# A hand-written order of operations in a fused attention and feed-forward kernel: the stretch behind the first batch's last scores is ordered anew, with weight sums in halves on two engines and two pairs turned by DMA

## The chip, the cores and the metric

The kernel runs on one core of a Trainium2 chip. The core has five engines with a queue of instructions each: TensorE (PE: matrix products; its weight loads are shown apart as PEld), VectorE (DVE), ScalarE (ACT), GpSimd (POOL) and SyncE (SP, which here issues most DMAs). Each queue runs in its own order and waits on semaphores for the others. The metric is device time in microseconds (us) for one execution.

## The reference

Eight batches of twelve heads, sequence 448, head size 64. Queries and keys are divided by their norms, the attention is a softmax of their products over tau, and its result goes through a feed-forward layer with a hard-swish:

```python
q_n = q / (norm(q) + 1e-06);  k_n = k / (norm(k) + 1e-06)
attn = softmax(q_n @ k_n.T / tau)
x = (attn @ v) as [3584 tokens, 768]
h = x @ w_in                       # 768 x 2048
g = h * clip(h + 3, 0, 6) / 6
out = g @ w_out                    # 2048 x 768
```

## The kernel before

The work is cut into 48 pairs of heads, six pairs to a batch. A pair i needs its queries and keys squared (SQ), the squares summed (RE), norms made of the sums (NO), inputs multiplied by them (NM), and the result turned so that the head's 64 values lie on partitions (TR by TensorE, XD by a transposing DMA); then copies of queries and keys (CQ, CK, CS), scores in four groups (SC), exponentials (EX), products with the values (VA) and a division (FI). The finished pair is turned back into the layout of x, by matmuls against an identity (BK, then a copy CX) or by a DMA: XB for one pair, XP for two. When six pairs of a batch are there, sixteen units of the first product (U: `mm1_unit`, L560) make g, each with a ScalarE step (UA) and a VectorE product (UV); the output units (`mm2_unit`, L606, six for batch 0; `product_unit`, L720, and `single_unit`, L810, later) make the result. An output unit of the first kind is sixteen matmuls, a bank of PSUM, and a copy into o (L624 on ScalarE, L626 on VectorE), which a DMA stores.

TensorE's work of the later batches uses fewer products by a Strassen-like scheme (L652 on). It needs sums of quarters of w_out: sums 1, 6 and 7 go to tiles of their own, y3 and y4 overwrite the right and the left columns of w_out in place (`weight_sums`, L673; one token, WS). So y3 may only run when the first three output units of batch 0, which read the right half, are done, and y4 after the last three. Before the change, all of these sums run on VectorE, sum 7 and y4 in two halves, the others whole.

The order of the first 18 pairs is written out by hand as text, `PLAN` (L21): each token is an operation, then its numbers, and often the engine (v VectorE, a ScalarE, p GpSimd) and a part. Instructions enter their engine's queue in the order of the tokens. DP and D are dummy matmuls (L921, L916). W issues the next of eight weight loads from GpSimd's queue: four pieces of w_in, then four of w_out (L907). LQ and LV load queries or keys and values from SyncE's queue. The tile `big` holds the raw inputs in seven places that come around, so a load waits for the normalisation of the item seven before. From pair 18 on (`FIRST`) a loop sets the order (L996 to L1050). Scores, first-layer units and output units share six PSUM banks in a ring (`next_bank`, L157): a matmul into a bank waits until whoever read its last content is done.

The change's own names: `norms` (L244) takes four ScalarE steps, a logarithm, a half power by Exp, a logarithm of that plus epsilon and an Exp of its negative; `back` (L483) and `copy_x` (L497) turn a pair by TensorE; `back_two` (L514) turns two by one DMA; `weight_sums` (L673); `vcast` (L278) turns values to bf16; `copy_k` (L350) and `copy_k3` (L364) copy keys out of PSUM.

Of the kernel before, what the change touches and what calls it, by code (L numbers as in the profile page):

```python
# [10 lines left out]
AF = mybir.ActivationFunctionType  # L11
# [3 lines left out]
EPS = 1e-6  # L15
# [42 lines left out]
]  # L58


# [1 line left out]
def kernel(  # L62
# [10 lines left out]
    nc = tc.nc  # L73
    B, H, S, D = q.shape
# [29 lines left out]
    KC = FCN // 2  # L104
# [34 lines left out]
    def raw_buffer(j):  # L139
# [4 lines left out]
    n2s = [const.tile([128, 2, 14], FP32, name=f"n2{i}", tag=f"n2{i}") for i in range(2)]  # L144
    rs = [
        [const.tile([128, 2, 14], FP32, name=f"{x}{i}", tag=f"{x}{i}") for x in ("ln", "nr", "le", "r")]
        for i in range(2)
    ]
# [13 lines left out]
    engines = {"v": nc.vector, "p": nc.gpsimd, "a": nc.scalar, "s": nc.sync}  # L162
    issued = set()

    def needs(*what):
        for w in what:
            assert w in issued or any(x < 0 for x in w[1:] if isinstance(x, int)), w
# [76 lines left out]
    def norms(d, *items):  # L244

        needs(("NM", 2 * d - 4), ("NM", 2 * d - 3))
        items = items or (0, 1)
        for x in items:
            needs(("RE", 2 * d + x))
        it = slice(items[0], items[-1] + 1)  # L250
        ln, nr, le, r = (t[:, it, :] for t in rs[d % 2])
        nc.scalar.activation(out=ln, in_=n2s[d % 2][:, it, :], func=AF.Ln)
        nc.scalar.activation(out=nr, in_=ln, func=AF.Exp, scale=0.5)
        nc.scalar.activation(out=le, in_=nr, func=AF.Ln, bias=EPS)
        nc.scalar.activation(out=r, in_=le, func=AF.Exp, scale=-1.0)  # L255
        for x in items:
            issued.add(("NO", d, x))

# [411 lines left out]
            return wide[n % 2], wide[2]  # L670
        return wide_late[2 * (n - LOOP) : 2 * (n - LOOP) + 2]

    def weight_sums(what, c0, n):  # L673

        w = w_out_sb[:, :, :].rearrange("p (c k) m -> p c k m", k=2)[:, c0 : c0 + n]
        b11, b12, b21, b22 = (w[:, :, k, m] for k in range(2) for m in (LEFT, RIGHT))
        for x in {"y3": "16", "y4": "17"}.get(what, ""):
            assert all((x, c) in summed for c in range(c0, c0 + n))
        o, x, y, op = {
            "1": (b11, b11, b22, ALU.add),  # L680
            "6": (b11, b11, b12, ALU.add),
            "7": (b21, b21, b22, ALU.add),
            "y3": (b12, b12, b22, ALU.subtract),
            "y4": (b21, b21, b11, ALU.subtract),
        }[what]
        if what in w_sum:
            o = w_sum[what][:, c0 : c0 + n, :]
        nc.vector.tensor_tensor(out=o, in0=x, in1=y, op=op)
        summed.update((what, c) for c in range(c0, c0 + n))

    def half(b, t, k):
# [146 lines left out]
    def halved(x):  # L838
        return [(weight_sums, x, c, KC // 2) for c in (0, KC // 2)]

    def products(text):
# [18 lines left out]
    APART = {(n, y) for n in range(len(PAIRS)) for x, y in (("5a", "3"), ("2a", "4")) if f"{x}.{n}" in " ".join(TURNS.values()).split()}  # L860
    side = {
        18: [(weight_sums, "y4", KC // 2, KC // 2)], 19: sums(0, "62"), 20: sums(0, "1"),
        21: sums(1, "75"), 22: sums(1, "621"),
        25: sums(2, "75"), 26: sums(2, "62"), 27: sums(2, "1"), 28: [(g_left, 2)], 29: sums(2, "e"),
# [7 lines left out]
    for b in range(2, B - 1):  # L872
        first = firsts(b, *range(FCN))
        for n, x in enumerate([0, 3, 3, 3, 3, 2]):
# [6 lines left out]
            x = 0 if n == 1 else 1 if n in (0, 5) and i > FIRST else 2  # L881
# [54 lines left out]
    def finish_units(e):  # L936
        post[e].pop(0)()

    def whole_units(n, engines="av"):
# [4 lines left out]
                    finish_units(e)  # L944

    OPS = {
        "LQ": load_qk, "LV": load_v, "W": next_weights, "SQ": square, "RE": reduce, "NO": norms,
        "NM": normalise, "VC": vcast, "TR": transposes, "XD": crossbar, "XB": back_crossbar, "XP": back_two, "CQ": copy_q, "CK": copy_k, "CS": copy_k3, "SC": scores,
        "EX": exps, "VA": values, "FI": finish_values, "BK": back, "CX": copy_x, "U": unit, "UA": lambda: finish_units("a"), "UV": lambda: finish_units("v"),
        "GL": g_left, "WS": lambda x, *h: weight_sums(str(x), *((h[0] * KC // 2, KC // 2) if h else (0, KC))), "UU": whole_units, "D": busy, "DP": busy_pv, "OPEN": open_ring,  # L950
    }

    def do(op, *args):
        OPS[op](*args)
        key = (op,) + tuple(a for a in args if isinstance(a, int))
        if op not in ("RE", "NM", "LQ"):
            issued.add(key[:3] if op == "SC" else key)

    def run(text):
        for t in text.split():  # L960
            op, *args = t.split(".")
            do(op, *(int(a) if a.lstrip("-").isdigit() else a for a in args))
# [20 lines left out]
    SC = [psum_s.tile([128, 2, 512], FP32, name=f"SC{n}", tag=f"SC{n}") for n in range(2)]  # L983
# [10 lines left out]
    if FIRST + 6 < NP:  # L994
        do("LQ", FIRST + 6)
    for i in range(FIRST, NP):  # L996
# [5 lines left out]
        def prepare(*what):  # L1002
            for op, n, *args in what:
                if n < (NP // 2 if op in ("NO", "LV") else NP):
                    do(op, n, *args)
# [27 lines left out]
        n = 2  # L1033
# [59 lines left out]
```

## Time and profile before

| | us |
|---|---|
| median of three runs | 405.38 (405.06 to 406.32) |
| profiled execution, whole | 405.02 |
| its span | 403.2 |
| TensorE busy | 394.5 |
| VectorE busy | 286.4 |
| ScalarE busy | 266.2 |
| GpSimd busy | 233.2 |

The span runs from the first to the last recorded instruction; the execution's own time has some 1.8 us around it. A stretch by stretch view gives each engine's busy time (x its instructions), the granted TensorE clock, the busy share of the DMA engines (several DMAs in flight count as more than 1) and GB/s. In the stretches that the change touches:

```profile
core 0: us, PE busy (x) PEld busy (x) DVE busy (x) ACT busy (x) POOL busy (x), PEclk, DMA share, GB/s
...
62.00:72.00 10.00, 10.00 (x123) 6.26 (x121) 7.94 (x19) 8.20 (x20) 5.92 (x4) 1.00 1.24 241
72.00:82.00 10.00, 10.00 (x83) 5.17 (x81) 8.38 (x14) 7.35 (x19) 4.64 (x7) 1.00 0.88 141
82.00:92.00 10.00, 10.00 (x103) 5.41 (x102) 5.90 (x11) 8.05 (x17) 6.76 (x7) 1.00 0.80 125
92.00:102.00 10.00, 10.00 (x95) 6.02 (x93) 7.45 (x12) 7.35 (x19) 4.15 (x6) 1.00 1.12 242
102.00:112.00 10.00, 10.00 (x90) 6.16 (x89) 9.60 (x14) 5.96 (x16) 2.33 (x2) 1.00 0.94 171
112.00:117.00 5.00, 3.99 (x41) 2.20 (x39) 5.00 (x4) 2.60 (x7) 4.86 (x5) 1.00 0.81 238
```

A row of a timeline gives the start, the time, the engine, the line, the operation with its tiles, its shapes and how many were merged; in brackets the engine's idle time before it and who ended that.

### The profile page before, as it was taken

Reading aid. Unit: us, or ns where it says so; the run is one execution under the profiler, and the core shown is the slowest. Engines: PE = TensorE matmul, PEld = TensorE weight load, DVE = VectorE, ACT = ScalarE, POOL = GpSimd, SP = SyncE. Lnnn points to the kernel's source line nnn. Section 1 sums busy time; section 2 is a strip of 40 time slices with the busy share of each in tenths; the row PEclk is TensorE's granted clock in tenths of the full one; section 3 lists DMA queues with packets and bytes.
Section 4 is the critical chain, followed back from the end, with each engine's and each line's share of the span. In section 5 each row is a group of like instructions: output and inputs, shape, how many; then the busy total and the mean of one; then the engine's idle time right before and its main releaser. Section 6 shows DMA issues by size and latency. Waiting matters only on the chain.

```text
span 403.2 us, 9617 instructions
## 1 busy us (share of the span) xinstructions
PE 394.5 (98%) x3696; PEld 233.7 (58%) x3696; DVE 286.4 (71%) x501; ACT 266.2 (66%) x609; POOL 233.2 (58%) x228
## 2 busy tenths in 40 slices
PE   7999999999989999999999999999999999999996
PEld 5666556555655556555555556555565556555564
DVE  6898768766998676776857878687656666644663
ACT  6899998787557686776758768668648755224230
POOL 7899664562294996489386875776665500510070
PEclk9999999999999999999999999999999999999999
DMA  8999989989989559885989659986864523130133
GB/s 290 308 241 276 200 249 239 144 126 221 193 204 231 120 119 228 176 224 130 181 214 210 134 143 171 183 193 145 191 150 82 112 46 67 40 79 20 27 73 99
DMA packets 91566, 65.32 MB, mean 162 GB/s; under 512 B 56064, under 2 KB 89984, under 8 KB 91520
## 3 DMA queue, kind: packets, MB, share of 16 engines
q1 hardware_dynamic: 87408, 58.02, 62.8%
q0 software_dynamic: 3712, 6.29, 9.1%
q8 instruction: 29, 0.48, 0.5%
q10 hardware_dynamic: 400, 0.39, 0.3%
q14 instruction: 17, 0.14, 0.1%
HBM read 47.19 MB, written 11.01 MB: 144 GB/s over the span
## 4 chain that ended last, share of the span: by engine, by line
PE 94%; DVE 3%; DMA 1%; POOL 1%; ACT 0%; issue 0%; SPq 0%; DVEq 0%
PE M L566 24%; PE M L739 17%; PE PV L455 13%; PE Y L566 6%; PE M L415 6%; PE Z L566 5%; PE Y L739 4%; PE Z L739 4%; PE M L613 3%; PE M L819 2%; PE Z L415 2%; PE PV L921 2%; PE Z L819 1%; PE Y L415 1%; PE SC L415 1%; DMA big<-in_q_dram 1%
## 5 line engine op out<-in xcount | busy, mean ns | idle before, releaser
L433 ACT ACTIVATE at<-M 128x448 bf16<-128x448 f32 x200 | 99.6, 565 | 17.7 <-PE M L415 15.5
L566 PE MATMUL M<-xT,w_in_sb 128*128 128x448 bf16 x522 | 110.7, 353 | 0.0
L566 PEld LDWEIGHTS <-w_in_sb 128*128 128x128 bf16 x768 | 71.9, 98 | 62.5 <-issue 2.6
L267 POOL TENSOR_TENSOR nrm<-big,r 128x896 bf16<-128x896 f32 (+1 forms) x48 | 79.4, 1658 | 26.7 <-ACT r L255 18.5
L581 DVE SCALAR_TENSOR_TENSOR gT<-u,M 128x448 bf16<-128x448 bf16 x76 | 46.8, 618 | 35.6 <-ACT u L575 35.3
L455 PEld LDWEIGHTS <-at 128*128 128x128 bf16 (+1 forms) x1536 | 54.8, 97 | 24.1 <-issue 14.8
L224 POOL TENSOR_TENSOR big<-big 128x896 f32<-128x896 f32 (+3 forms) x39 | 63.8, 1639 | 8.0 <-DMA big<-in_k_dram 4.1
L575 ACT ACTIVATE u<-M 128x448 bf16<-128x448 f32 x87 | 48.8, 561 | 29.5 <-PE M L566 29.1
L455 PE MATMUL PV<-vx,at 128*128 128x65 bf16 (+1 forms) x1536 | 64.3, 194 | 0.2 <-DVE on L476 0.2
L236 DVE TENSOR_REDUCE n<-big 128x14 f32<-128x896 f32 (+1 forms) x50 | 51.8, 1040 | 3.9 <-ACT big L222 3.4
L372 POOL COPY km<-tT 64x128 bf16<-64x128 bf16 x34 | 12.4, 364 | 59.3 <-DMA tT<-nrm 43.4
L768 POOL TENSOR_TENSOR big<-big 128x384 f32<-128x384 f32 x11 | 12.0, 1088 | 55.1 <-ACT big L787 55.0
L739 PEld LDWEIGHTS <-gT 128*128 128x128 bf16 x288 | 27.8, 98 | 20.2 <-DVE gT L717 0.6
L739 PE MATMUL M<-w_out_sb,gT 128*128 128x384 bf16 x208 | 37.9, 326 | 0.1
L433 ACT ACTIVATE at<-Z 128x448 bf16<-128x448 f32 x49 | 27.6, 564 | 10.4 <-PE M L415 8.8
L286 POOL CAST vx<-big 128x512 bf16<-128x512 f32 x44 | 33.0, 754 | 2.4 <-DMA big<-in_v_dram 2.4
L476 DVE TENSOR_TENSOR on<-PV,rc 128x512 bf16<-128x512 f32 x48 | 33.2, 691 | 1.7
L415 PE MATMUL M<-tT,kz 64*128 64x448 bf16 (+1 forms) x175 | 31.9, 351 | 1.0 <-DVE o L626 1.0
L739 PEld LDWEIGHTS <-gs 128*128 128x128 bf16 x224 | 21.6, 98 | 14.5
L566 PE MATMUL Y<-xT,w_in_sb 128*128 128x448 bf16 x132 | 28.6, 353 | 0.0
L433 ACT ACTIVATE at<-Y 128x448 bf16<-128x448 f32 x45 | 25.6, 568 | 3.3 <-PE Z L415 3.1
L739 PE MATMUL M<-w_sum,gs 128*128 128x384 bf16 x144 | 26.3, 326 | 0.0
(131 smaller groups left out, 553.9 us busy)
## 6 DMA issues: line engine op xcount, KB each, us to landing
big<-in_v_dram SPq DMA_DIRECT2D x96, 128.0 KB, 4.7
big<-in_k_dram SPq DMA_DIRECT2D x24, 448.0 KB, 4.9
big<-in_q_dram SPq DMA_DIRECT2D x24, 448.0 KB, 4.3
out_dram<-o SPq DMA_DIRECT2D x107, 96.0 KB, 2.2
w_in_sb<-in_moe_w_in_dram POOLq DMA_DIRECT2D x4, 768.0 KB, 9.1
w_out_sb<-in_moe_w_out_dram POOLq DMA_DIRECT2D x4, 768.0 KB, 9.7
tT<-nrm SPq DMA_TRANSPOSE x34, 3.4
xT<-on SPq DMA_TRANSPOSE x25, 3.8
```

The source lines that it names most:

```text
L224: engines[e].tensor_tensor(out=o, in0=i, in1=i, op=ALU.mult)
L236: nc.vector.tensor_reduce(out=n2s[d % 2][:, j % 2, c], in_=sq[:, :, :, :].rearrange("p g c d -> p (g c) d")[:, c, :], axis=AX.X, op=ALU.add,)
L267: engines[e].tensor_tensor(out=nrm[:, :, g, :].rearrange("p c g d -> p g c d"), in0=raw_of[j][:, g, :, :], in1=rs[d % 2][3][:, j % 2, :] . ...
L286: (engines[e].copy if e == "a" else engines[e].tensor_copy)(out=o, in_=f)
L415: nc.tensor.matmul(o, ks, qt[rows], start=True, stop=True)
L433: nc.scalar.activation(out=o, in_=x, func=AF.Exp, scale=inv_tau)
L455: nc.tensor.matmul(pv_out(j, h), at[rows, n, q_cols(i // HP, j)], vt[rows, 3 + h if name == "M" else 5 * h + int(name[1]), :], start=(name ...
L476: nc.vector.tensor_tensor(out=on[:, :, :, :].rearrange("p j h d -> p h j d"), in0=pv4[:, :, :, 0:D], in1=rc[:, :, :].to_broadcast([128, 2, ...
L566: nc.tensor.matmul(ps[:, 0:S], w_in_sb[:, cc, fc * 128 : (fc + 1) * 128], x[:, cc, 0:S], start=(cc == 0), stop=(cc == CC - 1),)
L575: nc.scalar.activation(out=u[:, :], in_=ps[:, 0:S], func=AF.Relu, bias=0.5, scale=1.0 / 6.0)
L581: nc.vector.scalar_tensor_tensor(out=g[:, fc, c0 : c0 + S], in0=u[:, :], scalar=1.0, in1=ps[:, 0:S], op0=ALU.min, op1=ALU.mult,)
L739: nc.tensor.matmul(m, lhs[:, c, :], rhs[:, c, c0 : c0 + width], start=(base is None and c == 0), stop=(c == KC - 1), skip_group_check=True,)
```

## The change

`PLAN` is the same up to the keys' copies of pair 6; from there to its end (pairs 4 to 17 in their several stages) it is written anew. In it:

- The three dummy matmuls of this stretch (DP.2, two of them, behind OPEN, and DP.1 behind CK.9) are gone.
- Pairs 8 and 9 of batch 1 are turned by one DMA, XP.8; before, by BK.8 and BK.9 on TensorE with copies CX.8 on VectorE and CX.9 on ScalarE.
- Norms 5 and 8 are made by NA (two ScalarE steps, `powers`) and ND (two VectorE steps, `reciprocals`) in the place of the four ScalarE steps.
- Weight sums name an engine and are all in halves: lower halves of 1 and 6 on GpSimd near pair 13, the upper halves of 7, 6 and 1 on VectorE near pairs 15 and 16, both halves of y3 on GpSimd and the lower halves of 7 and y4 on VectorE near pair 17. Before, all on VectorE, sum 6 first near the end of pair 15.
- Other operations change engine: the copies CS.8, CS.9, CS.12, CS.13, CK.10, CK.13 and CX.10 and the value casts VC.12 and VC.18 go to ScalarE, CK.12 from it to VectorE; the casts VC.7, 13, 14, 16, 17 and 19 and the normalisations 12 and 19 go from GpSimd to VectorE; squares 13, 15 and the last part of 16 go from ScalarE to GpSimd, 18 from ScalarE to VectorE, 19 from GpSimd and 22 from VectorE to ScalarE.
- Weight loads W three and four come earlier, five and six later; loads LQ.13, LQ.15 and LQ.19 come later.
- The tokens of scores, values, units and their finishing steps are interleaved differently; the order of the loop from pair 18 on is the same.

```diff
-    "BK.3.Y VA.4.1 LQ.12 CS.6.v OPEN DP.2 CX.3.v NO.5 SC.6.0 VA.4.2 VA.4.3 SC.6.1 SC.6.2 EX.6.0 NM.8.p FI.4 EX.6.1",
...
-    "U UA EX.11.0 LV.7 EX.11.1 UV UA SC.11.2 RE.15 BK.8 LQ.18 CX.8.v U VA.10.0 U VA.10.1 UA EX.11.2 UV UV RE.14",
-    "SC.11.3 UA BK.9 VA.10.2 VA.10.3 FI.10 EX.11.3 TR.13 NO.7 CK.13.v CS.13.v CX.9.a U UV CK.12.a VC.11.p W",
...
-    "CK.17.v XD.18 U EX.16.1 SQ.20.a.0.7 NM.19.p FI.15 WS.6 U UV XD.19 SC.16.3 RE.20 GL.0 WS.1 WS.7.0 EX.16.2 U VA.16.0 UA VA.16.1 LV.11",
-    "EX.16.3 SC.17.0 UV VC.19.p SC.17.1 SC.17.2 SQ.22.v.0.7 VA.16.2 LQ.23 EX.17.0 VA.16.3 EX.17.1 LV.10 U SC.17.3",
-    "XP.14 NO.10 FI.16 NM.20.p CK.18.v U CK.19.v WS.7.1 WS.y3 WS.y4.0 XB.16 EX.17.2 UV UA VA.17.0 VC.18.p EX.17.3 RE.22 CS.18.v",
+    "BK.3.Y VA.4.1 LQ.12 CS.6.v OPEN CX.3.v SC.6.0 VA.4.2 NA.5 NM.8.p EX.6.0 VA.4.3 SC.6.1 FI.4 SC.6.2 TR.8",
+    "SC.6.3 CQ.9.v EX.6.1 BK.4 CQ.8.v W VA.5.0 VA.5.1 VA.5.2 EX.6.2 EX.6.3 SC.7.0 VA.5.3 NM.9.p EX.7.0 CX.4.v",
+    "SC.7.1 FI.5 SC.7.2 VC.6.p VC.8.p TR.9 W SC.7.3 EX.7.1 VA.6.0 BK.5 VA.6.1 CS.8.a ND.5 CX.5.v NM.11.p U",
...
+    "UV VA.10.3 UA TR.13 TR.12 SQ.17.p.0.7 EX.11.3 NO.7 UV U FI.10 CQ.12.v CS.12.a BK.10 CQ.13.v CS.13.a UV",
+    "CK.13.a VA.11.0 VA.11.1 UA VA.11.2 CK.12.v SC.12.0 SC.12.1 CX.10.a LQ.16 NM.14.p SQ.16.p.0.7 UV SC.12.2 XP.8",
+    "VC.13.v EX.12.0 VA.11.3 U FI.11 EX.12.1 U UA NM.15.p SC.12.3 RE.17 BK.11 EX.12.2 EX.12.3 CX.11.v UV VA.12.0",
+    "W RE.16 LQ.18 UA VC.15.p U XD.14 UA UV U U NA.8 UA SQ.18.v.0.7 UV U RE.18 UA LQ.19 SC.13.0 EX.13.0 ND.8",
+    "NM.16.p U UA W UV UA WS.1.p.0 UV VA.12.1 UV UV W U VC.14.v U UA WS.6.p.0 UA SC.13.1 SC.13.2 UV VA.12.2 U",
...
+    "VA.15.0 UV LQ.22 EX.15.2 WS.7.v.1 CK.17.v LQ.20 XP.12 VA.15.1 SC.16.0 WS.6.v.1 EX.15.3 UA VC.16.v SC.16.1",
+    "GL.0 SC.16.2 VA.15.2 EX.16.0 RE.21 NM.19.v VA.15.3 U EX.16.1 SC.16.3 LV.9 EX.16.2 U SQ.20.a.0.7 U FI.15",
+    "WS.1.v.1 XD.18 VC.17.v LV.11 UV WS.y3.p.1 XD.19 UA RE.20 EX.16.3 WS.y3.p.0 VA.16.0 VA.16.1 SC.17.0 LQ.23 UV",
+    "SC.17.1 SC.17.2 XP.14 SQ.22.a.0.7 VC.19.v EX.17.0 VA.16.2 EX.17.1 VA.16.3 U WS.7.v.0 FI.16 NO.10 SC.17.3 UA",
+    "CK.18.v XB.16 RE.22 U EX.17.2 NM.20.p VA.17.0 WS.y4.v.0 LV.10 VC.18.a UV EX.17.3 CK.19.v CS.18.v",
@@
+    def powers(d, *items):
...
+        nc.scalar.activation(out=ln, in_=n2s[d % 2][:, it, :], func=AF.Ln)
+        nc.scalar.activation(out=nr, in_=ln, func=AF.Exp, scale=0.5)
...
+    def reciprocals(d, *items):
...
+        nc.vector.tensor_scalar_add(out=le, in0=nr, scalar1=EPS)
+        nc.vector.reciprocal(out=r, in_=le)
@@
-    def weight_sums(what, c0, n):
+    def weight_sums(what, c0, n, e="v"):
...
-        nc.vector.tensor_tensor(out=o, in0=x, in1=y, op=op)
+        engines[e].tensor_tensor(out=o, in0=x, in1=y, op=op)
```

More of the change, by code (lines that the diff above doesn't have):

```diff
@@ L255, in norms @@
         nc.scalar.activation(out=r, in_=le, func=AF.Exp, scale=-1.0)
+        for x in items:
+            issued.add(("NO", d, x))
+    def powers(d, *items):
+        needs(("NM", 2 * d - 4), ("NM", 2 * d - 3))
+        items = items or (0, 1)
+        for x in items:
+            needs(("RE", 2 * d + x))
+        it = slice(items[0], items[-1] + 1)
+        ln, nr = (t[:, it, :] for t in rs[d % 2][:2])
+        nc.scalar.activation(out=ln, in_=n2s[d % 2][:, it, :], func=AF.Ln)
+        nc.scalar.activation(out=nr, in_=ln, func=AF.Exp, scale=0.5)
+        for x in items:
+            issued.add(("NA", d, x))
+    def reciprocals(d, *items):
+        items = items or (0, 1)
+        for x in items:
+            needs(("NA", d, x))
+        it = slice(items[0], items[-1] + 1)
+        nr, le, r = (t[:, it, :] for t in rs[d % 2][1:])
+        nc.vector.tensor_scalar_add(out=le, in0=nr, scalar1=EPS)
+        nc.vector.reciprocal(out=r, in_=le)
         for x in items:
@@ L946 @@
     OPS = {
-        "LQ": load_qk, "LV": load_v, "W": next_weights, "SQ": square, "RE": reduce, "NO": norms,
+        "LQ": load_qk, "LV": load_v, "W": next_weights, "SQ": square, "RE": reduce, "NO": norms, "NA": powers, "ND": reciprocals,
         "NM": normalise, "VC": vcast, "TR": transposes, "XD": crossbar, "XB": back_crossbar, "XP": back_two, "CQ": copy_q, "CK": copy_k, "CS": copy_k3, "SC": scores,
         "EX": exps, "VA": values, "FI": finish_values, "BK": back, "CX": copy_x, "U": unit, "UA": lambda: finish_units("a"), "UV": lambda: finish_units("v"),
-        "GL": g_left, "WS": lambda x, *h: weight_sums(str(x), *((h[0] * KC // 2, KC // 2) if h else (0, KC))), "UU": whole_units, "D": busy, "DP": busy_pv, "OPEN": open_ring,
+        "GL": g_left, "WS": lambda x, e, *h: weight_sums(str(x), *((h[0] * KC // 2, KC // 2) if h else (0, KC)), e), "UU": whole_units, "D": busy, "DP": busy_pv, "OPEN": open_ring,
     }
@@ L955, in do @@
         key = (op,) + tuple(a for a in args if isinstance(a, int))
-        if op not in ("RE", "NM", "LQ"):
+        if op not in ("RE", "NM", "LQ", "NA", "ND"):
             issued.add(key[:3] if op == "SC" else key)
```

28 rows, old and new, of the table PLAN are left out of this document.

## The prediction

> **What bounds the kernel now.** I read the page's shares first, then TensorE's waits, then the timeline of each engine around the longest wait inside the changed stretch.
>
> ```profile
> PE 394.5 (98%) x3696; PEld 233.7 (58%) x3696; DVE 286.4 (71%) x501; ACT 266.2 (66%) x609; POOL 233.2 (58%) x228
> ...
> PEclk9999999999999999999999999999999999999999
> ```
>
> TensorE is busy for 394.5 of 403.2 us at the full granted clock. No other engine comes near, so a moved operation costs nothing until TensorE waits for it, and a matmul taken out saves its whole time.
>
> ```profile
> PE PV L921 <- DVE vx L972: 2.5, 1, 2.5
> PE M L415 <- DVE o L626: 1.0, 1, 1.0
> PE Z L312 <- POOL nrm L267: 0.7, 1, 0.7
> ```
>
> The first and third waits lie in the first 11 us, which the change leaves alone. The second lies in the changed stretch (about 35 to 120 us): a score matmul of pair 18.
>
> ```profile
> 115.03 0.35 PE L415 MATMUL M<-tT,kz 64*128 64x448 bf16 x1
> 116.39 0.35 PE L415 MATMUL M<-tT,kz 64*128 64x448 bf16 x1 [1.01 <-DVE o L626]
> ```
>
> Start to start that is 1.36 us where 0.19 is usual: 1.17 lost. The bank it writes still held an output tile, whose copy (L626) stood behind the weights' sums on VectorE:
>
> ```profile
> 110.48 0.95 DVE L688 TENSOR_TENSOR w_sum<-w_out_sb 128x1536 bf16<-128x1536 bf16 x1
> 111.34 4.52 DVE L688 TENSOR_TENSOR w_out_sb<-w_out_sb 128x3072 bf16<-128x3072 bf16 x2
> 115.79 0.54 DVE L626 COPY o<-M 128x384 f32<-128x384 f32 x1
> ```
>
> ```profile
> 111.00 1.97 POOL L267 TENSOR_TENSOR nrm<-big,r 128x896 bf16<-128x896 f32 x1 [7.67 <-ACT r L255]
> 112.92 2.14 POOL L286 CAST vx<-big 128x512 bf16<-128x512 f32 x1
> ```
>
> (The row at 111.34 merges two sums: y3, 3.24 us, and half of y4, 1.36.) GpSimd's cast takes 0.61 us elsewhere and 2.14 here: it ends 0.5 us after y3 does, so it ran only then. And y3, begun under a normalisation, took 3.24 us, against 1.75 for a sum as long with GpSimd idle (104.57). So a sum on VectorE and an operation on GpSimd exclude each other for their whole length. The key copies (L362) overlap GpSimd freely at 0.34 us. This decides what follows.
>
> **What goes from TensorE.** Three dummy matmuls (L921) at 0.106 us apart: 0.32. The two turns BK.8 and BK.9, four matmuls each, 0.19 to 0.21 a block (61.09 to 61.30): 0.39. Scores come closer together:
>
> ```profile
> 60.80 0.36 PE L415 MATMUL Z<-tT,kz 64*128 64x448 bf16 x1
> 61.09 0.37 PE L495 MATMUL M<-ident,on 128*128 128x128 bf16 x4
> 61.30 1.30 PE L566 MATMUL M<-xT,w_in_sb 128*128 128x448 bf16 x6
> ...
> 98.18 0.35 PE L415 MATMUL Y<-tT,kz 64*128 64x448 bf16 x1
> 98.37 0.35 PE L415 MATMUL Z<-tT,kz 64*128 64x448 bf16 x1
> ```
>
> A pair of score matmuls holds TensorE for 0.29 us when something else follows, 0.19 when another pair does. By the two orders 23 pairs of the stretch are followed by something else before, 18 after: 5 x 0.10 = 0.5. Together 1.2 us. Bounds: 0.7 (removed matmuls alone) to 1.5.
>
> **What stalls go.** The 1.17 above, and 0.17 at 120.85, where an output matmul waits on a product queued behind the last half sum (118.46, 2.13 us): 1.34. Sum saved: 2.5 us.
>
> **What is added or moved.**
> The weight sums. Before: seven sums on VectorE (L688) from 100.2 on. After: four halves go to GpSimd (the lower halves of sums 1 and 6 near pair 13, both halves of y3 near pair 17), and five stay on VectorE, apart from y4's upper half, which comes later in both. The trace has no bf16 sum on GpSimd. Its nearest rows:
>
> ```profile
> L224 POOL TENSOR_TENSOR big<-big 128x896 f32<-128x896 f32 x36 | 60.8, 1691 | 6.8 <-DMA big<-in_k_dram 3.3 <-DVE n L236 1.3 <-DVE on L476 0.9
> L780 POOL TENSOR_TENSOR o<-o,big 128x384 f32<-128x384 f32 x5 | 4.9, 997 | 0.3 <-ACT o L776 0.3
> L224 POOL TENSOR_TENSOR big<-big 128x768 f32<-128x768 f32 x1 | 1.5, 1457 | 0.0
> ```
>
> Squares, whose two inputs are one tensor, go from 1.46 (768) to 1.68 (896): 1.73 ns an element and 0.13 fixed, so 2.8 us for 1536. With two different inputs, as here, 384 take 0.997; times four is 4.0, with the same fixed part 3.6. Bounds for a half, P: 2.7 to 4.0; I take 3.2, between the row of like inputs and the row of like length.
>
> An estimate from the Trainium skill (GPSIMD Engine Reference, Performance versus the Vector engine): 2.6 cycles an element for two inputs at 1.2 GHz is 3.3 us; by that the new stall below is 0.8 instead of 0.6 and the time 404.2. The page's Engine selection speaks against the move (elementwise work belongs on VectorE, about 2x slower here); the rows agree (0.95 against 2.7 to 4.0), but TensorE only feels what is late.
>
> What is late next. Let T be the end of the third right-half output unit; the first y3 half starts on GpSimd then, the second ends at T+2P. VectorE's WS.7 half comes up between and waits for T+2P. Behind it, by start spacings: WS.7 0.9, FI.16 0.85, CK.18 0.27, RE.22 1.02, half of y4 0.81 (1.36 at 114.51 less 0.55 behind a cast), the copy that frees the bank 0.56: T+2P+4.4. TensorE needs that bank after three output units (3 x 2.60), the scores of 17 (0.66+0.19), five value groups (1.2) and two pairs of 18 (0.38): T+10.2. P=2.9 breaks even, each 0.1 more costs 0.2. At P=3.2: 0.6 us; bounds 0 and 2.2.
>
> The sums on GpSimd near pair 13 hold up its next in line: the weight load W behind the first, km's copies (CS.14) and a normalisation behind the second, then XD.16, whose buffer km's copies free. In the trace XD.16 lands 6.6 us after issue. I find about 1 us to spare before SC.16; price nothing, 0 to 1.
>
> Weight loads. The last (84.70 before) is issued about when it was and has 3 us to spare before the first output unit at 95.0. The second (28.01 on POOL, 12.2 to landing) arrives at 40.2; the first unit moves ahead of value groups 6.2 and 6.3, SC.8 and a dummy (1.66 us), from 42.09 to about 40.1: wait 0.15, bounds 0 and 0.8.
>
> XP.8 puts one transposing DMA (about 1.3 us on SP's queue, 3.6 to landing) in the place of eight matmuls, one VectorE cast (0.62) and one ScalarE cast (0.51). It waits for FI.9; behind it stand LQ.18 and XD.14, both waiting for normalisations anyway. xT is needed some 7 us later: nothing. Loads LQ.13, 15 and 19 come later, each squared later too: nothing, up to 0.5 where the queue is crowded.
>
> Norms 5 and 8: two ScalarE steps (0.23 each) become an add and a reciprocal on VectorE. Small rows: 0.065 (a fill) to 0.21 (L475), up to 1.7 if the add must wait for GpSimd. VectorE sits idle 2.25 us before 44.85; price nothing.
>
> Pair 12 and 13's last key blocks and VC.12 go to ScalarE (0.48 and about 0.6 by L332 and L222). VectorE's CK.12 then waits for ScalarE, and with it a product that frees a bank for SC.12: 0.3 us, bounds 0 and 0.6. Six value casts (0.68 by L284) and two normalisations (1.09, L267) go from GpSimd to VectorE, 6.3 us, and four half sums (3.6) leave it: 2.7 more over 80 us in which it idles about a quarter. Squares trade places. Banks that are freed a little later for it: 0.1, up to 0.5.
>
> **Sum.** Against the profiled execution (403.2 span, 405.02 whole): -2.5 +0.6 +0.15 +0.3 +0.1 = -1.35 us, so 401.9 and 403.7. Its time is 0.36 under the median of 405.38 of the runs; on the median: 404.0.
>
> **Rivals.**
> Cheap GpSimd: P=2.7, as with the squares. No stall at pair 18: 405.38-2.5+0.55 = 403.4. For it: bf16 reads half the bytes. Against: the 384 rows.
> Dear GpSimd: P=4.0. Stall 2.2 takes the place of 1.17: 405.38-2.5+0.55+2.2 = 405.6, no change. For it: L780. Against: no other row is that dear per element.
> Slower: the upper half of sum 1, last of VectorE's sums before y3, slips behind y3's first half. It has 2.6 us to spare: TensorE takes 11.3 us from SC.15's third pair to T, VectorE 8.7 for its queue up to that sum. If XD.16 (held by GpSimd, then 5 to 7 us in flight) or a landing of values makes VectorE later than that, the sum waits P, and then the cast VC.17 (0.6) and an output copy (0.5) behind it: TensorE needs its bank at T+3.1 and gets it at T+P+2, 2.1 late; WS.7 later by another 0.9. With the forecast: 407.0. For it: long landings (5.6 to 6.6) at 87 to 99. Against: 2.6 is more than any one delay I find.
> The change does nothing it says: banks or buffers move the wait, 405.4.
>
> **How the numbers follow.** Forecast 0.52, own range 403.2 to 405.0; cheap 0.13; dear 0.14; slipped 0.18; nothing 0.03. 0.3% is 1.2 us, about what a measurement here tells from no change: the line lies at 404.2. Faster: cheap 0.13 and two thirds of the forecast, 0.48; slower: slipped 0.18 and 0.04 of dear, 0.22; within: the rest, 0.30. The range goes from 402.8 (2.5 saved, no new stall) to 407.0 (slipped).
>
> **What would show it.** Right: eleven matmuls fewer; no 1 us wait at pair 18's scores, or one of 0.5 to 0.8 behind L626; GpSimd's sums near 3.2 us; WS.7 on VectorE stretched to 3 us or more. Wrong: P outside 2.7 to 4.0, a wait at the first hidden unit over 0.8, or sum 1's upper half lasting over 2 us.

## The result, and the profile after

The changed kernel is slower: 412.21 us (408.80 to 414.72, 4 runs) against 405.85 for the kernel before in the same measurement, a ratio of 1.0138 with a 95% interval of 1.0100 to 1.0177. Ratios and their intervals leave out executions over 1.5% slower than the fastest of the same kernel (none here, up to three of ten below) and the medians do not, so the two can differ. The profiled execution took 412.3 us with a span of 410.3, 7.1 more than before. The page, then TensorE's waits (us in total, times, longest):

```profile
PE 397.5 (97%) x3685; PEld 235.2 (57%) x3685; DVE 286.5 (70%) x501; ACT 267.3 (65%) x614; POOL 238.9 (58%) x223
...
PEclk9999999998999899999999999999999999999999
```

```profile
PE M L592 <- DMA xT<-on: 3.1, 1, 3.1
PE M L441 <- POOL km L398: 2.7, 1, 2.7
```

TensorE has eleven matmuls fewer and is yet busy for 3.0 us longer. The 1.0 us wait at pair 18 is gone, and two longer ones have come. The stretches show where the busy time grew:

```profile
90.00:95.00 5.00, 2.29 (x35) 1.37 (x33) 3.20 (x5) 1.91 (x5) 4.86 (x4) 1.00 0.97 157
95.00:100.00 5.00, 5.00 (x27) 2.44 (x26) 0.93 (x3) 3.51 (x8) 2.79 (x4) 0.66 1.14 119
...
133.00:137.00 4.00, 4.00 (x15) 1.73 (x13) 1.76 (x4) 1.93 (x7) 3.35 (x4) 0.58 0.97 250
```

The columns are busy time of PE, PEld, DVE, ACT and POOL with their instructions, the granted clock, the DMA share and GB/s. TensorE's rows at the two waits:

```profile
93.87 0.36 PE L441 MATMUL M<-tT,km 128*128 128x448 bf16 x1 [2.71 <-POOL km L398]
...
95.40 2.42 PE L592 MATMUL M<-xT,w_in_sb 128*128 128x448 bf16 x6
...
132.47 4.30 PE L592 MATMUL M<-xT,w_in_sb 128*128 128x448 bf16 x13 [3.12 <-DMA xT<-on]
```

Behind each wait the granted clock falls (0.66 and 0.58 as means of the two stretches) and matmuls of 448 columns start 0.37 us apart instead of 0.19. Start to start, the waits cost 2.87 and 3.29 us over the usual spacing and the slow stretches 1.6 each: 9.4. Against it stand the 1.34 of waits and the 1.2 of TensorE's work that the prediction counted as saved: 6.8 of the 7.1.

Where the first wait comes from is read from GpSimd's timeline, of the kernel before and then of the changed one:

```profile
59.15 0.74 POOL L909 DMA_DIRECT2D w_out_sb<-in_moe_w_out_dram  x1
...
84.12 0.64 POOL L372 COPY km<-tT 64x128 bf16<-64x128 bf16 x2
```

```profile
71.01 0.81 POOL L935 DMA_DIRECT2D w_out_sb<-in_moe_w_out_dram  x1
...
79.32 0.80 POOL L935 DMA_DIRECT2D w_out_sb<-in_moe_w_out_dram  x1
85.42 3.08 POOL L714 TENSOR_TENSOR w_sum<-w_out_sb 128x1536 bf16<-128x1536 bf16 x1 [5.29 <-DMA w_out_sb<-in_moe_w_out_dram]
88.46 0.78 POOL L935 DMA_DIRECT2D w_out_sb<-in_moe_w_out_dram  x1
89.26 3.10 POOL L714 TENSOR_TENSOR w_sum<-w_out_sb 128x1536 bf16<-128x1536 bf16 x1
92.30 1.51 POOL L398 COPY km<-tT 64x128 bf16<-64x128 bf16 x2
```

The load issued at 71.01 is the second quarter of w_out (59.15 before). Sum 1's lower half needs it, and GpSimd, in order, stands still for 5.29 us until it lands at 85.3. Behind that sum wait the last weight load, sum 6's lower half, and then the copies of pair 14's last keys (CS.14), which start at 92.30 (84.12 before). TensorE wants them at 91.0 for SC.14's last score and gets them at 93.8.

The second wait comes in part from the same copies; the experiments below show another part. The copies free the buffer that XD.16 fills, and XD.16 stands at the head of SyncE's queue, which had issued nothing since 72.9. From there to the transpose that TensorE misses:

```profile
93.84 3.87 SPq L349 DMA_TRANSPOSE tT<-nrm  x2
...
121.17 1.23 SPq L533 DMA_TRANSPOSE xT<-on  x1
122.45 3.85 SPq L208 DMA_DIRECT2D big<-in_v_dram  x4
...
128.33 1.22 SPq L533 DMA_TRANSPOSE xT<-on  x1
```

SyncE then issues with no gap over 0.15 us from 95.6 until XB.17 is out. XB.16 goes out at 121.17, and XB.17 only at 128.33, though pair 17's product was ready at 120.9: LV.10's four loads, two outputs and LQ.24 stand ahead. In the kernel before, XB.17 went out at 121.45:

```profile
121.45 1.21 SPq L507 DMA_TRANSPOSE xT<-on  x1
```

Batch 2's first unit runs five of its six matmuls, the fifth at 128.99, and stops there until XB.17 lands at 132.4.

### The profile page after: what moved, and what is told of

Its sections match the earlier page's. It is cut to its first block, busy times and chain, and to the rows that moved or that the text cites. A ratio compares the mean times of both kernels' runs of the same rounds, so it can differ in the third digit from the quotient of the medians.

```text
span 410.3 us, 9609 instructions
## 1 busy us (share of the span) xinstructions
PE 397.5 (97%) x3685; PEld 235.2 (57%) x3685; DVE 286.5 (70%) x501; ACT 267.3 (65%) x614; POOL 238.9 (58%) x223
## 4 chain that ended last, share of the span: by engine, by line
PE 84%; POOL 5%; DMA 4%; DVE 3%; issue 1%; ACT 1%; POOLq 0%
PE M L592 20%; PE M L765 16%; PE PV L481 11%; PE M L441 5%; PE Y L765 4%; PE Z L592 4%; PE Y L592 4%; PE Z L765 3%; DMA w_out_sb<-in_moe_w_out_dram 3%; PE PV L947 3%; PE M L845 3%; PE M L639 2%; POOL big L225 2%; POOL w_sum L714 2%; PE Y L441 1%; PE Z L845 1%
## 5 line engine op out<-in xcount | busy, mean ns | idle before, releaser
L592 PE MATMUL M<-xT,w_in_sb 128*128 128x448 bf16 x552 | 119.0, 359 | 3.1 <-DMA xT<-on 3.1
L459 ACT ACTIVATE at<-M 128x448 bf16<-128x448 f32 x193 | 96.3, 566 | 24.1 <-PE M L441 14.2
L607 DVE SCALAR_TENSOR_TENSOR gT<-u,M 128x448 bf16<-128x448 bf16 x82 | 50.3, 618 | 39.6 <-ACT u L601 39.3
L601 ACT ACTIVATE u<-M 128x448 bf16<-128x448 f32 x92 | 51.5, 561 | 35.1 <-PE M L592 34.8
L225 POOL TENSOR_TENSOR big<-big 128x896 f32<-128x896 f32 (+2 forms) x40 | 65.8, 1646 | 12.2 <-DMA big<-in_q_dram 4.7
L459 ACT ACTIVATE at<-Y 128x448 bf16<-128x448 f32 x52 | 29.5, 567 | 6.3 <-PE Z L441 4.9
L765 PE MATMUL M<-w_out_sb,gT 128*128 128x384 bf16 x176 | 32.4, 326 | 0.1
L312 POOL CAST vx<-big 128x512 bf16<-128x512 f32 x36 | 25.1, 698 | 9.1 <-DMA big<-in_v_dram 4.6
L765 PE MATMUL M<-w_sum,gs 128*128 128x384 bf16 (+1 forms) x160 | 27.7, 318 | 0.0
L592 PE MATMUL Z<-xT,w_in_sb 128*128 128x448 bf16 x126 | 27.3, 353 | 0.0
```

What stands on the lines that cost most here:

```text
L225: engines[e].tensor_tensor(out=o, in0=i, in1=i, op=ALU.mult)
L312: (engines[e].copy if e == "a" else engines[e].tensor_copy)(out=o, in_=f)
L459: nc.scalar.activation(out=o, in_=x, func=AF.Exp, scale=inv_tau)
L592: nc.tensor.matmul(ps[:, 0:S], w_in_sb[:, cc, fc * 128 : (fc + 1) * 128], x[:, cc, 0:S], start=(cc == 0), stop=(cc == CC - 1),)
L601: nc.scalar.activation(out=u[:, :], in_=ps[:, 0:S], func=AF.Relu, bias=0.5, scale=1.0 / 6.0)
L607: nc.vector.scalar_tensor_tensor(out=g[:, fc, c0 : c0 + S], in0=u[:, :], scalar=1.0, in1=ps[:, 0:S], op0=ALU.min, op1=ALU.mult,)
```

## The experiments

Each is the changed kernel with one edit, unless it says otherwise; the ratio is to the kernel before. PLAN's fragments stand for the lines that hold them.

### The two sums, later on GpSimd

```diff
-W UV UA WS.1.p.0 UV VA.12.1 UV UV W U VC.14.v U UA WS.6.p.0 UA
+W UV UA UV VA.12.1 UV UV W U VC.14.v U UA UA
-RE.21 NM.19.v
+RE.21 WS.1.p.0 WS.6.p.0 NM.19.v
```

> The two half sums of 1 and 6 stay on GpSimd but move from ahead of pair 14's last-key copies (CS.14) to the 8.6 us in which GpSimd idles before y3. Theory A (one cause: these sums, standing where they do, hold back CS.14 and through it XD.16 and SyncE's whole queue): both of TensorE's waits go, the 2.7 us at SC.14's last score and the 3.1 us for XB.17's transpose, and with them the two stretches at half clock (about 1.6 us each): 412.2 - 2.7 - 3.1 - 3.2 = 403.2; 402.5 to 404.5. Theory B (two causes: the second wait comes from LV.10, which now stands between XB.16 and XB.17 on SyncE): only the first wait and its half clock go, 412.2 - 4.3 = 407.9; 407 to 409.

Measured: 413.81, ratio 1.0158 (1.0108 to 1.0208). Both theories missed. The two waits did go, but a new one of 5.5 us came, from an effect that the prediction had named and I then left out: an operation on VectorE beside one on GpSimd. Behind the new wait the granted clock is 0.5 from 111.0 to 121.2 us. GpSimd and VectorE, and the TensorE row that waits:

```profile
104.07 6.31 POOL L714 TENSOR_TENSOR w_out_sb<-w_out_sb 128x1536 bf16<-128x1536 bf16 x2 [0.95 <-PE M L639]
104.45 2.99 DVE L583 COPY gT<-gT 128x1024 bf16<-128x1024 bf16 x1
108.36 2.97 DVE L293 TENSOR_TENSOR nrm<-big,r 128x896 bf16<-128x896 f32 x1
112.22 1.04 PE L481 MATMUL PV<-vx,at 128*128 128x65 bf16 x16 [5.55 <-DVE on L502]
```

The same copy took 0.42 us, the same normalisation 1.08, with GpSimd idle. Beside sums on GpSimd each ends only after the sum beside it (the first sum ends at 107.2, the second at 110.4), and pair 15's division, behind them, is 5.5 us late. So GpSimd's 8.6 idle us before y3 were no free place: what fills them is paid by VectorE.

### LV.10 ahead again

```diff
-SC.17.1 SC.17.2 XP.14
+SC.17.1 SC.17.2 LV.10 XP.14
-WS.y4.v.0 LV.10 VC.18.a
+WS.y4.v.0 VC.18.a
```

> Only LV.10's four loads move back on SyncE's queue, ahead of XP.14, where the kernel before has them. Theory A: the queue is full without a gap from 95.6 to 129.6 us, so XB.17 is issued at the same time (128.3): the 3.1 us wait stays at 2 to 3.3, both stretches at half clock stay, 411 to 412.5. Theory B: XB.17 is issued 3.9 us earlier, the second wait and its half clock go: 412.2 - 4.7 = 407.5.

Measured: 407.51 (404.67 to 413.15), ratio 0.9989 (0.9947 to 1.0031). The median is theory B's 407.5, but by luck: B had the second wait gone. This settled neither theory, but its profile gave the clue: nothing ahead of pair 16 was edited, and yet the first wait is not in it.

```profile
80.70 3.10 POOL L714 TENSOR_TENSOR w_sum<-w_out_sb 128x1536 bf16<-128x1536 bf16 x1
...
87.58 0.64 POOL L398 COPY km<-tT 64x128 bf16<-64x128 bf16 x2
```

Here the second w_out load, issued at 71.55, had landed by 80.7, so sum 1 started at once and CS.14 at 87.58, in time. The same transfer took 14.3 us in the one profile and 8.7 in the other. A wait for xT of 2.0 us stays although SyncE started on time: without the first wait TensorE reaches the unit at 123.96, and XB.17 is issued at 123.15, 1.7 later than in the kernel before.

### The wait filled with dummies

```diff
-VA.14.1 SC.14.3
+VA.14.1 DP.26 SC.14.3
```

> 26 dummy matmuls (0.106 us each, 2.76 in all) stand ahead of SC.14's last score, so TensorE works through the wait. Clock theory (the half clock after 95.4 follows from the idle 2.7 us): the granted clock stays 1.0 from 90 to 100 us and that stretch is 1.6 us shorter; the second wait, for a transpose whose issue depends on SyncE and not on TensorE, then grows by up to 1.6 us, so the time lies between 410.6 and 412.2. Rival (the clock falls for load or by a timer of its own): the clock is below 0.9 from 95 to 100 as before, time 412.2 or a little more.

Measured: 410.10, ratio 1.0075 (1.0041 to 1.0109). TensorE's stretch from 95 us:

```profile
95.00:100.00 5.00, 5.00 (x47) 2.89 (x44) 2.18 (x5) 3.98 (x10) 2.20 (x3) 1.00 0.89 153
```

The load landed late here too (sum 1 starts at 84.98), but the clock stays at 1.00 where it was 0.66, and 47 matmuls fit where 27 did. So the fall of the clock follows from the idle time, as the clock theory said. The time is a little under its range: the second wait did not grow as I expected (2.2 us against 3.1), and no slow stretch followed it.

### The kernel before with the two sums alone

```diff
-VA.13.0 VC.14.p CS.14.v
+VA.13.0 VC.14.p WP.1 WP.6 CS.14.v
-FI.15 WS.6 U
+FI.15 WS.6.1 U
-GL.0 WS.1 WS.7.0
+GL.0 WS.1.1 WS.7.0
+"WP": lambda x: weight_sums(str(x), 0, KC // 2, "p")
```

(`weight_sums` also takes the engine, as in the changed kernel.)

> The kernel before with one part of the change: the lower halves of sums 1 and 6 on GpSimd ahead of CS.14, and off VectorE. Theory A: CS.14 starts about 6.2 us later (90.3 for 84.1), SC.14's last score waits about 3 us (due at 87.9, ready at 91), and half clock follows (up to 1.6 us); the 1.2 us wait at pair 18 may go as VectorE has 1.9 us less to do. 405.4 + 3 + 1.6 - (0 to 1.3) = 408.5 to 410. Theory B (the sums as such are harmless, it was the late landing of the second weight load, which here lands at 74.7): no wait at SC.14, 404 to 405.4.

Measured: 411.97, ratio 1.0109 (1.0053 to 1.0165). GpSimd, then TensorE:

```profile
86.59 6.13 POOL L688 TENSOR_TENSOR w_sum<-w_out_sb 128x1536 bf16<-128x1536 bf16 x2
92.66 0.63 POOL L372 COPY km<-tT 64x128 bf16<-64x128 bf16 x2
```

```profile
93.35 0.56 PE L415 MATMUL M<-tT,km 128*128 128x448 bf16 x1 [2.82 <-POOL km L372]
```

Theory A's wait, 2.8 us for the 3 forecast, with half clock behind it. In this order the sums alone are too long, with no late landing. The 1.0 us wait at pair 18 stayed and 0.4 for xT came. The median lies above the forecast of 408.5 to 410, the ratio (4.4 us on 405.4) inside it. The profiled execution was 2.5 us late already ahead of the edit (GpSimd's normalisation before the sums starts at 84.38 for 81.92), so its span is no measure.

### The second w_out load early again

```diff
-XP.6 W LV.7
+XP.6 W W LV.7
-"W RE.16 LQ.18
+"RE.16 LQ.18
```

> Only the second load of w_out moves: issued right behind the first, as in the kernel before, 12 us earlier than in the changed kernel. Theory A (the first wait is the length of two half sums on GpSimd plus the 5.3 us in which GpSimd, in order, waits for this load to land): it lands by 75, sum 1's half starts at about 80.9, CS.14's copies at 87.6, the wait at SC.14 goes in every run; SyncE's queue starts moving again at about 88 instead of 93.8. The second wait shrinks but stays at 1 to 2 us, as LV.10 is still ahead of XB.17: 405 to 407.5. Rival (the length of the sums alone is enough): CS.14 still late by 2 us or more, 409 to 412.

Measured: 406.06 (404.91 to 412.06), ratio 1.0018 (0.9998 to 1.0038). Moving one load by 12 us takes back nearly the whole loss. In the profile the first wait is gone, and 2.1 us for xT are left, as theory A had it:

```profile
79.95 3.10 POOL L714 TENSOR_TENSOR w_sum<-w_out_sb 128x1536 bf16<-128x1536 bf16 x1
...
86.83 0.64 POOL L398 COPY km<-tT 64x128 bf16<-64x128 bf16 x2
```

```profile
PE M L592 <- DMA xT<-on: 2.1, 1, 2.1
```

The load took 12.8 us to land here too; it is safe because it starts at 61.1. In the new order CS.14 is needed later than in the old one, so with an early landing the two sums do not stall it. How the loss splits is not shown, though: moving LV.10 alone, as above or as below, also gives a ratio near 1 (0.9989, 1.0007), and in the one profile of each the load had landed in time.

### LV.10 behind XB.17

With the early load, and alone:

```diff
-WS.y4.v.0 LV.10 VC.18.a
+WS.y4.v.0 VC.18.a
...
             do("XB", i - 1)
+            if i == FIRST:
+                do("LV", 10)
```

> The same, and LV.10's four loads go behind XB.17 on SyncE. Theory A2 (XB.17's landing is what TensorE waits for at batch 2's first unit, and it is late because of the issues ahead of it on SyncE): XB.17 is issued 2.6 us earlier than in e2 (120.5 for 123.15) and lands at about 124.4, due at 124.7: no wait over 0.3, no half clock: e2's span of 404.9 - 2.0 - 1.3 = 401.6, time 403.5; 402.8 to 404.5. Rival (pair 17's own product, or the output copies ahead of it on the queue, hold XB.17): a wait of 1 to 2 us stays, 405 to 407.

> Only LV.10 moves behind XB.17; the second load of w_out stays late. Theory A: where that load lands late (85.3 in the changed kernel) the first wait and its half clock stay and the second shrinks from 3.1 to 0.7 or less: about 408; where it lands early (before 80.7, as in e2) neither is left: about 403.5. Between, by the landing: median 406 to 408.5, and a spread of some 4 us. Rival: as the changed kernel, 411 to 412.5.

Measured: 405.89, ratio 1.0009 (0.9996 to 1.0022), with the early load; 405.62 (403.73 to 410.83), ratio 1.0007 (0.9976 to 1.0039), without. With the early load XB.17 went out at 118.61, even before the 120.5 expected, and the wait for xT shrank to 0.2. But the time did not follow: a third wait came up. GpSimd, VectorE and TensorE of the first of the two:

```profile
135.28 0.99 POOL L795 TENSOR_TENSOR big<-big,o 128x384 f32<-128x384 f32 x1
136.31 0.56 DVE L822 TENSOR_TENSOR big<-M,big 128x384 f32<-128x384 f32 x1 [1.96 <-POOL big L795]
136.92 1.46 PE L765 MATMUL M<-w_sum,gs 128*128 128x384 bf16 x8 [1.43 <-DVE big L822]
```

A bank is freed by an addition (L822) that needs the end of a chain on GpSimd: pair 20's key copies at 127.19, as soon as XD.20's transpose lands, then a square, a normalisation, a cast and four additions. XD.20 was issued at 123.59, behind LV.10. Ahead of the key copies GpSimd also stands still for 8.2 us at pair 20's value cast, which waits for LV.10 itself and starts at 126.27. The run without the early load shows the same wait (1.0 us). Its median is under the 406 to 408.5 expected; its spread of 7 us is what a landing now early, now late would give, but only one execution was profiled, and there the load landed in time (9.0 us).

### Sums 1 and 6 whole on VectorE

```diff
-WS.1.p.0, WS.6.p.0
-WS.6.v.1
+WS.6.v
-WS.1.v.1
+WS.1.v
```

This goes on top of the early load and LV.10 behind XB.17.

> As e6, with sums 1 and 6 whole on VectorE instead of their lower halves on GpSimd; y3 stays on GpSimd. VectorE has 1.9 us more to do before y3. Theory (my own count gave VectorE 2.6 us to spare there): no new wait, CS.14 at about 82, time as e6 within 0.5: 403 to 404.5. Rival (the half sums on GpSimd earn their place, VectorE's queue is full at pairs 15 to 17): a new wait of 0.5 to 2 us behind VectorE, 404.5 to 406.

Measured: 405.99, ratio 1.0032 (1.0009 to 1.0054). CS.14 now starts at 81.3, and VectorE causes no wait at pairs 15 to 17; the time falls into the rival's range, but for another reason: the wait behind L822 is 1.9 us. So the sums on VectorE are not the bound; a ratio of 1.0032 against 1.0009 with overlapping intervals shows no clear loss by them.

### XD.20 ahead of LV.10

```diff
         elif even:
             do("XP", i - 2)
         if even:
             prepare(("XD", i + 2))
+        if i == FIRST:
+            do("LV", 10)
...
-        prepare(("NM", i + 3, "p"), ("VC", i + 2, "p"))
+        prepare(("NM", i + 3, "p"))
+        if i == FIRST + 1:
+            prepare(("VC", i + 1, "a"))
+        if i > FIRST:
+            prepare(("VC", i + 2, "p"))
```

Pair 20's value cast, which GpSimd would wait at, goes to ScalarE one pair later. Three kernels: with the early load; with the sums on VectorE instead; with both.

> The second w_out load early as in e5, and on SyncE XB.17 and then XD.20 go ahead of LV.10's loads; pair 20's value cast, which waits for LV.10, leaves GpSimd's queue for ScalarE one pair later. Theory C (the 1.4 us wait of e6 at 135, for a bank that product 1 frees, is GpSimd's chain behind XD.20's landing: CS.20, square, normalisation, cast, four additions): XD.20 is issued 3.6 us earlier than in e6 (119.9 for 123.6), CS.20 starts by 124 instead of 127.2, and neither the wait for xT nor the one at 135 is left over 0.3 us: e6's span 402.8 - 1.6 = 401.2, time 403.0; 402.4 to 404, faster than both kernels. Rival (GpSimd's or ScalarE's own load, not the landing, sets that chain): a wait of 0.8 us or more stays near 135, 404.5 to 406.

> The same SyncE order with the second w_out load left late and sums 1 and 6 whole on VectorE. Theory A: without sums on GpSimd near pair 13 nothing waits for that load before the first output unit (95), so its late landing costs nothing: no wait at SC.14, time as e9 within 0.6: 402.6 to 404.2. Rival (VectorE is full, or the last w_out load lands late): a wait of 0.5 to 2 us between 94 and 118, 404 to 406.

> Both: the second w_out load early and sums 1 and 6 whole on VectorE, with the SyncE order of e9. Theory: as e9 within 0.4, so the half sums of 1 and 6 on GpSimd are worth nothing by themselves: 402.6 to 404.2. Rival: they relieve VectorE at pairs 15 to 17, this is 0.5 to 1.5 us slower than e9.

Measured: 404.09, ratio 0.9968 (0.9946 to 0.9991); 403.62, 0.9955 (0.9935 to 0.9975); 403.77, 0.9944 (0.9918 to 0.9969). All three are faster than the kernel before, by 0.3 to 0.6%, and so than the changed one. Their intervals overlap, so the half sums of 1 and 6 on GpSimd are worth nothing that these runs can show. All of TensorE's waits over 0.1 us in the first:

```profile
PE PV L947 <- DVE vx L998: 2.5, 1, 2.5
PE PV L481 <- DVE on L502: 0.2, 1, 0.2
```

No wait is left in the changed stretch, and its span is 400.5, 2.7 under the kernel before; this is the quickest of its twelve executions. XD.20 and the cast were not tried apart. In the run with LV.10 ahead of XD.20 the key copies needed both the end of the cast (126.9) and the landing of XD.20 (127.1), so by these two times moving one alone would have gained 0.2 us (an estimate). The other two profiles have a wait of 1.3 us at the first unit, for the second of w_in's four pieces. In the one with the load left late, that load took 14.3 us again, and nothing waited for it.

### Two value groups ahead of the first unit

```diff
-VA.6.1 CS.8.a ND.5
+VA.6.1 VA.6.2 VA.6.3 CS.8.a ND.5
-EX.8.1 VA.6.2
+EX.8.1
-UA VA.6.3 SC.8.2
+UA SC.8.2
```

This goes on top of the last of the three.

> e11 with value groups 6.2 and 6.3 (0.66 us of TensorE) back ahead of the first hidden unit. Theory: that unit waits for the second half of w_in to land (1.3 us in the profiles of e10 and e11, 0 in e9's), and TensorE has this work to do meanwhile: the wait shrinks by 0.66 where there is one, and nothing changes where there is none: the ratio to the kernel before falls from 0.9944 to about 0.993, 403.0 to 403.7. Rival (the landing moves as the transfers around it do, or the moved groups cost a wait of their own): 0.994 to 0.997.

Measured: 403.60, ratio 0.9955 (0.9924 to 0.9985). The wait for w_in is not in its profile, but the ratio did not fall: no gain shown. Whether the landing of w_in decides anything in most executions stays open.

## Why the prediction was wrong

It forecast 404.0; 412.2 was measured. The savings were right, and two answers to "what is late next" were wrong.

- **Saved, 2.5 us: right.** Eleven matmuls are gone, and the waits at pair 18 too. Where no new wait follows, the span is 2.7 shorter (400.5 for 403.2), in the quickest of twelve executions; by the ratios the last three kernels gain 1.3 to 2.3 us.
- **P, a half sum on GpSimd, 3.2 us: right.** 3.08 to 3.11. Sum 7's half on VectorE was stretched to 3.23, as said, and pair 18's bank came back in time: 0 for the 0.6 forecast.
- **"price nothing, 0 to 1" for the sums near pair 13: this step failed.** It cost 2.7 us of wait and 1.6 of half clock, and it made SyncE's queue 5 us late. I had the queue right (the load, CS.14, XD.16 behind the sums) but priced it as if both sums started when issued and as if only XD.16 waited. I never asked when the sum's own input lands: the front text says that loads five and six come later, and my step on weight loads followed only the second and the last. And CS.14's copies are themselves read by SC.14's last score. The last load, "issued about when it was", also stood in that queue: 88.46 for 84.70. The early load alone took the ratio from 1.0138 to 1.0018; that the sums alone can stall CS.14 is shown in the order of the kernel before (a wait of 2.8 us).
- **"the sum" as a gain in the time: failed a second time, at batch 2's first unit.** I subtracted 2.5 us from the end without asking what TensorE would reach earlier. XB.17 was issued at 121.45 in the kernel before, for a unit that began at 125.77; TensorE 2 us ahead meets it unlanded (2.0 and 2.1 us in the two profiles without the first wait). LV.10's move on SyncE behind XB.16 I did not price at all. Once it was out of the way, GpSimd's chain behind XD.20 took its place.
- **The first hidden unit, 0.15 (0 to 0.8):** 0.17 start to start in the changed kernel, 1.3 to 1.5 in three later profiles: bounds too narrow. SC.12's 0.3 is not seen.
- **The slower rival, sum 1's upper half slipping behind y3, did not happen** (0.95 us, at 106.50). The loss came from the lower halves, on the other engine.

## What to carry to other kernels

When an operation moves to another queue, price it from the later of its place in that queue and the landing of its inputs, and follow everything behind it to its first reader on the bounding engine. Where the bounding engine gains time, list the transfers that it will meet earlier: here 2.5 us saved went into one wait after another until the orders on GpSimd's and on SyncE's queue had both been changed. An idle stretch of GpSimd is not free while VectorE works on sums, normalisations or large copies.

## What the runs showed of the hardware

- A wait of TensorE costs more than its length. After idle stretches of 2.7, 2.8 and 3.1 us the granted clock was 0.5 for 3.4 us each time (1.6 us more each in the changed kernel), after 5.5 us for 10.2. After 2.0 us it fell in two profiles; after 1.9, 2.1 and 2.2 in three others it did not. The Trainium skill (TensorE: Matmul & The Clock Gate, HAM oscillation — how this bites in real kernels) warns of idle gaps over about 3.4 us; these runs show the drop at shorter ones, and here the measurement decides.
- A copy with one input on VectorE (L583, 128x1024 bf16) is held by a sum on GpSimd as well: 2.99 us for 0.42. The prediction had seen key copies run freely beside GpSimd; the trace before also has this copy beside a normalisation on GpSimd, at 193.59, where it takes 1.18. The Trainium skill (SBUF — State Buffer, Who interferes with whom) has the two engines share a pair of ports under a lock held for the whole instruction, and says that some copies take it; the 2.99 agrees.
- The same 768 KB load, with the same order of work ahead of it, took 13.3 to 15.0 us to land in four profiles and 8.7 and 9.0 in two. What delays it was not found.
